# A spectral and dense two-layer program on one core: the shared SBUF region moved by 32 bytes, two transposes and the W2 loads reordered

## The chip, the cores and the metric

The kernel runs on one core of a Trainium2 chip. The metric is the device time of one execution in microseconds (us). Times of single instructions come from one profiled execution.

## The reference

Input x has 2048 rows of 1024 bf16 numbers. The program applies a spectral layer A, a dense layer B, and both once more with the same weights; each adds its result to x:

```
x = x + A(layernorm(x));  x = x + B(layernorm(x))      # twice
A(x): irfft2(rfft2(x) * (w_r + 1j*w_i))                # 2048 x 513 complex weights
B(x): h = x @ w1 + b1                                  # 1024 x 3584
      (h * tanh(softplus(h))) @ w2                     # mish, then 3584 x 1024
```

## The kernel before, in words

x stays in SBUF as XS, 16 tiles of 128 rows. Everything else, in both layers, lives in one shared region, ARENA; `alloc` cuts buffers out of it by hand-written byte offsets, and a new buffer inherits the waits of what lay there. ARENA is the last tensor that `build` reserves, so its start follows from the sizes of the small tensors ahead of it, of which EPS (a constant for the square root and a scratch word) and PAD1 (not used) are the last two. `W1_OFF`, where the W1 ring and the filter ring lie, is counted back from the region's end.

Each engine has a program of its own in the order in which the Python code adds operations; the code works out which semaphores each must wait for. So the order of the text is the order on each engine and on each DMA queue. Most loads are issued by SyncE (SP).

Layer A is a Fourier transform made of matmuls. In the first application the normalised x is never written; x is loaded a second time in a transposed order (XR, 32 loads of 128 KB with rows of 256 bytes) and multiplied with tables scaled by each row's factor (MN, `scaled`). Stage by stage for 8 groups, s2, s3, i1 and i2 follow. The result of each group is written to DRAM (`u_scratch`) and read back transposed into UT, in rows of 256 bytes (`u_turn`, `u_back`). The last matmuls of layer A, `i4`, need all of UT; they belong to the dense layer's code and are mixed into it.

Layer B takes the 2048 rows as four chunks of 4 tiles, c = 0 to 3. For each tile a layernorm is made (statistics on VectorE or, with `stats_act` and `sums_to_mv`, on ScalarE; `scales` is a chain of small VectorE operations; `apply` writes the normalised tile xn). For chunks 0 and 1, `transposed` makes 8 TensorE transposes of a tile (L933) into one bank, and VectorE copies the bank to XT (L938). `mm1(c, fg)` is 2 x 8 matmuls (L963) with a W1 tile, into three banks in turn, each followed by ScalarE's Mish (L967); a third argument takes half of the chunk's columns. After an `mm1` of chunk 1 the next W1 tile is loaded over the one just read. `mm2(c, t, h)` sums 28 matmuls (L981) over all tiles of W2, and VectorE adds the bank to XS (L986).

Chunks 0 and 1 are worked on in rounds, fg = 5 to 16. Each round has an `mm1` of chunk 0 (to fg = 13), one of chunk 1 (three tiles behind), `rest(3)`, and up to three loads of W2 tiles. `rest(n)` does n of the 16 units of i4 that make XS tiles 8 to 15: unit nb is 8 small matmuls (L888) into bank 3 + nb % 3, emptied by VectorE (L902). W2 tiles 16 to 27 lie in space that is free; tiles 0 to 15 lie where UT is, so they are loaded only in rounds that come after the last unit:

```
            rest(3)
            for _ in range(3):
                if w2_order and (w2_order[0] >= 16 or self.nb == 16):
                    load_w2(w2_order.pop(0))
```

After the rounds the first `mm2` waits for all 28 tiles of W2. SyncE then also issues the transposes by DMA for chunks 2 and 3 (`turned`).

Of the kernel before, what the change touches and what calls it, by code (L numbers as in the profile page):

```python
# [9 lines left out]
F32 = dt.float32  # L10
# [164 lines left out]
def to_bf16_bits(a):  # L175
    u = np.ascontiguousarray(a, dtype=np.float32).view(np.uint32).astype(np.uint64)
    return np.ascontiguousarray((((u + 0x7FFF + ((u >> 16) & 1)) >> 16) & 0xFFFF).astype(np.uint16))


class KB:  # L180
# [122 lines left out]
    def build(self):  # L303
        nc = self.nc
        tabs = make_tables()
        con = {k: nc.inline_tensor(to_bf16_bits(v), name=f"c_{k.lower()}") for k, v in tabs.items()}
        self.con = {k: v.ap().bitcast(BF) for k, v in con.items()}
        self.con["IDF"] = nc.inline_tensor(np.eye(P, dtype=np.float32), name="c_idf").ap()
        self.u_d = nc.dram_tensor("u_scratch", (8, P, 16, P), BF, kind="Internal").ap()
        self.w_d = nc.dram_tensor("w_scratch", (8, P, 2, 2, 512), BF, kind="Internal").ap()  # L310
        self.xn_d = nc.dram_tensor("xn_scratch", (16, P, self.D), BF, kind="Internal").ap()
        from contextlib import ExitStack
        with ExitStack() as es:
            def sb(name, shape, dtype=BF):
                return es.enter_context(nc.sbuf_tensor(name, [P] + shape, dtype))

            sb("PAD0", [64])
            self.XS = sb("XS", [16, self.D])
            self.IDENT = sb("IDENT", [P])
            self.M = sb("M", [P])  # L320
            self.MT = sb("MT", [P])
            self.FD = sb("FD", [5 * 512])
            self.BD = sb("BD", [13 * P])
            self.B1 = sb("B1", [self.NF], F32)
            self.B1h = sb("B1h", [self.NF])
            self.BN = sb("BN", [16, 12], F32)
            self.MV = sb("MV", [16, 2], F32)
            self.RS = sb("RS", [4, 16], F32)
            self.EPS = sb("EPS", [2], F32)
            sb("PAD1", [92])  # L330
            self.PS = es.enter_context(nc.psum_tensor("PS", [P, 8, 512], F32))
            self.PSb = self.PS[:].bitcast(BF)
            self.arena_bytes = nc.sbuf_bytes_remaining // 64 * 64 - 64
            self.ARENA = es.enter_context(nc.sbuf_tensor("ARENA", [P, self.arena_bytes // 2], BF))
            self.r_bank = [Res(f"bank{i}") for i in range(8)]
            self.r_xs = [Res(f"XS{i}") for i in range(16)]
            self.r_mv = [Res(f"MV{i}") for i in range(16)]
            self.r_rs = [Res(f"RS{i}") for i in range(16)]
            self.r_ident, self.r_m, self.r_mt, self.r_fd, self.r_bd = (Res(n) for n in ("id", "m", "mt", "fd", "bd"))
            self.r_b1, self.r_eps, self.r_warm = Res("b1"), Res("eps"), Res("warm")  # L340
            self.r_ud = [Res(f"ud{i}") for i in range(8)]
            self.r_wd = [Res(f"wd{i}") for i in range(8)]
            self.r_xnd = [Res(f"xnd{i}") for i in range(16)]
            self.npair = 0
            self.W1_OFF = self.arena_bytes - 4 * 4096
            self.layout()
            self.prologue()
            self.layer_A(0)
            self.layer_B(0, last=False)
            self.layer_A(1)  # L350
            self.layer_B(1, last=True)
            self.dma_wait_all()
            for p in (self.pe, self.dve, self.act, self.sp, self.pool):
                p.sem = es.enter_context(nc.semaphore(name=f"sem_{p.name}"))
            for d_ in self.dsems.values():
                d_.sem = es.enter_context(nc.semaphore(name=d_.name))
            self.block = es.enter_context(nc.Block())
            self.flush()
# [557 lines left out]
    def layer_B(self, li, last):  # L916
# [6 lines left out]
        def transposed(c, t, xn, eng=None):  # L923
            bank = 6 + nt[0] % 2
            nt[0] += 1
            xn.unread = False
            if t == 0:
                if XT[c % 2] is None:
                    XT[c % 2] = self.alloc(f"XT{c % 2}", self.ob[f"XT{c % 2}"], [8, 512])
                XT[c % 2].res.begin()  # L930
            fns = []
            for db in range(8):
                fns.append(lambda e, db=db: e.transpose(PSb[:, bank, db * P:(db + 1) * P], xn.ap[:, db * P:(db + 1) * P],  # L933
                                                        self.IDENT[:]))
            self.group(fns, reads=[xn.res, self.r_ident], writes=[self.r_bank[bank]])
            dst = XT[c % 2].ap[:, :, t * P:(t + 1) * P]
            src = PSb[:, bank, :].rearrange("p (a b) -> p a b", b=P)
            fn = (lambda e: e.activation(dst, src, ACT.Copy)) if eng is act else (lambda e: e.tensor_copy(dst, src))  # L938
            self.op(eng or dve, fn, reads=[self.r_bank[bank]], parts=[XT[c % 2].res])
# [11 lines left out]
        def mm1(c, fg, half=None):  # L951
            n = base + 14 * (c // 2) + fg
            wb = self.w1_buf[n % 6]
            x = XT[c % 2]
            tok = slice(0, 512) if half is None else slice(256 * half, 256 * half + 256)
            w = tok.stop - tok.start
            for fl in range(2):
                ft = 2 * fg + fl
                bank = nh[0] % 3
                nh[0] += 1  # L960
                fns = []
                for db in range(8):
                    fns.append(lambda e, db=db, bank=bank, fl=fl: e.matmul(  # L963
                        PS[:, bank, 0:w], wb.ap[:, db, fl * P:(fl + 1) * P], x.ap[:, db, tok], start=(db == 0), stop=(db == 7)))
                self.group(fns, reads=[wb.res, x.res], writes=[self.r_bank[bank]])
                at, ra = AT[c % 2], r_at[c % 2][ft]
                self.op(act, lambda e, bank=bank, ft=ft: e.activation(at.ap[:, ft, tok], PS[:, bank, 0:w], ACT.Mish,  # L967
                                                                      bias=self.B1[:, ft:ft + 1]),
                        reads=[self.r_bank[bank], self.r_b1], writes=[ra])
            if c % 2 and half != 0 and self.w1_next == n + 6 and n + 6 < base + 28:  # L970
                self.load_w1()
# [36 lines left out]
        def load_w2(ft):  # L1008
            W2[ft] = self.alloc(f"W2_{ft}", self.ob["W2"] + ft * 2048, [self.D])
            self.dma(sp, W2[ft].ap, w2v[:, ft, :], f"w2_{ft % 4}", writes=[W2[ft].res])  # L1010
# [5 lines left out]
        xn = {}  # L1016
# [3 lines left out]
        def at_tiles(c):  # L1020
            off = self.ob[f"AT{c}"]
            AT[c] = self.alloc(f"AT{c}", off, [NF, 512])
            r_at[c] = [Res(f"AT{c}_{ft}") for ft in range(NF)]
            for ft, r in enumerate(r_at[c]):
                r.inherit(AT[c].res)
                self.live.append((off + ft * 1024, off + ft * 1024 + 1024, r))

        def rest(n):

            for _ in range(n):  # L1030
                if self.nb == 0:
                    for j in range(8, 16):
                        self.r_xs[j].begin()
                if self.nb < 16:
                    self.i4(8, 8, 8 * self.nb, 8, 3 + self.nb % 3)
                    self.nb += 1
# [37 lines left out]
        for fg in range(4):  # L1074
            mm1(0, fg, 1)
            if fg in (1, 3):
                self.stats_act(6 + fg // 2)
        self.sums_to_mv(6, 2)
        self.scales(6, 2)
        for j in (6, 7):  # L1080
            xn[j] = self.apply(j)
        mm1(0, 4)
        at_tiles(1)
        for j in (4, 5):
            transposed(1, j - 4, xn[j])
        for fg in range(2):
            mm1(1, fg, 0)
        for j in (6, 7):
# [5 lines left out]
        for fg in range(5, 14 + 3):  # L1094
            if fg < 14:
                mm1(0, fg)
            mm1(1, fg - 3)
            rest(3)
            for _ in range(3):
                if w2_order and (w2_order[0] >= 16 or self.nb == 16):  # L1100
                    load_w2(w2_order.pop(0))
# [68 lines left out]
```

## Time and profile before

| what | us |
|---|---|
| three runs: median (lowest, highest) | 1082.23 (1076.47, 1083.42) |
| the profiled execution | 1081.24 |
| its span, from the first to the last instruction | 1079.4 |
| TensorE busy in it (PE) | 959.7 |
| VectorE busy (DVE) | 350.9 |
| ScalarE busy (ACT) | 339.5 |

The span is cut into instructions by engine; us in all rows count from the span's start. Idle time of TensorE is what an edit can give back; idle time of the others costs nothing by itself. The mean granted clock of TensorE was 0.96 of full speed.

### The profile page before, as it was taken

Reading aid. Unit: us, or ns where it says so; the run is one execution under the profiler, and the core shown is the slowest. Engines: PE = TensorE matmul, PEld = TensorE weight load, DVE = VectorE, ACT = ScalarE, POOL = GpSimd, SP = SyncE. Lnnn points to the kernel's source line nnn. Section 1 sums busy time; section 2 is a strip of 40 time slices with the busy share of each in tenths; the row PEclk is TensorE's granted clock in tenths of the full one; section 3 lists DMA queues with packets and bytes.
Section 4 is the critical chain, followed back from the end, with each engine's and each line's share of the span. In section 5 each row is a group of like instructions: output and inputs, shape, how many; then the busy total and the mean of one; then the engine's idle time right before and its main releaser. Section 6 shows DMA issues by size and latency. Waiting matters only on the chain. (4 is left out here: it accounts for less than half of the span.)

```text
span 1079.4 us, 14332 instructions
## 1 busy us (share of the span) xinstructions
PE 959.7 (89%) x6063; PEld 521.2 (48%) x6153; DVE 350.9 (33%) x775; ACT 339.5 (31%) x504; POOL 64.1 (6%) x102
## 2 busy tenths in 40 slices
PE   0699478998999999999967984899989999999998
PEld 0588375543444444444425754654434444444443
DVE  7877463250343200023325775413401110000111
ACT  6798344332000233400006863533300013441000
POOL 2042000000000000000520200000000000000000
PEclk9899779998999999999988995999999999999999
DMA  9969941446111122000951798044621112200000
GB/s 280 153 221 277 176 119 40 155 157 203 44 46 40 40 78 59 1 10 20 197 96 21 199 206 185 1 138 154 220 59 36 53 46 78 79 1 10 20 20 30
DMA packets 158480, 107.04 MB, mean 99 GB/s; under 512 B 80432, under 2 KB 138032, under 8 KB 158416
## 3 DMA queue, kind: packets, MB, share of 16 engines
q1 hardware_dynamic: 146272, 77.57, 28.2%
q0 software_dynamic: 9056, 26.87, 9.6%
q10 hardware_dynamic: 3088, 1.67, 0.9%
q8 instruction: 49, 0.80, 0.3%
q14 instruction: 15, 0.12, 0.0%
HBM read 80.85 MB, written 20.71 MB: 94 GB/s over the span
## 5 line engine op out<-in xcount | busy, mean ns | idle before, releaser
L963 PE MATMUL PS<-ARENA 128*128 128x512 bf16 (+1 forms) x1946 | 392.4, 361 | 14.2 <-DVE ARENA L938 11.0
L981 PE MATMUL PS<-ARENA 128*128 128x512 bf16 x1756 | 388.4, 381 | 8.5 <-DMA ARENA<-in_B_w_dram 6.6
L967 ACT ACTIVATE ARENA<-PS,B 128x512 bf16<-128x512 f32 (+1 forms) x248 | 159.6, 645 | 449.8 <-PE PS L963 449.8
L963 PEld LDWEIGHTS PS<-ARENA 128*128 128x128 bf16 x1984 | 194.3, 99 | 205.4 <-DVE ARENA L938 12.6
L981 PEld LDWEIGHTS PS<-ARENA 128*128 128x128 bf16 x1792 | 175.9, 98 | 220.8 <-issue 11.5
L986 DVE TENSOR_TENSOR XS<-PS,XS 128x512 bf16<-128x512 f32 x64 | 44.3, 692 | 517.0 <-PE PS L981 517.0
L453 DVE BATCH_NORM_STATS2 BN<-XS 128x6 f32<-128x512 bf16 x104 | 67.2, 675 | 7.5 <-DMA XS<-in_A_x_dram 6.3
L902 DVE TENSOR_TENSOR XS<-PS,XS 128x512 bf16<-128x512 f32 (+1 forms) x40 | 29.5, 791 | 110.8 <-PE PS L888 110.8
L888 PE MATMUL PS<-MT,ARENA 128*128 128x32 bf16 (+1 forms) x768 | 23.9, 187 | 32.7 <-DMA ARENA<-u_scratch 30.5
L888 PEld LDWEIGHTS PS<-MT,ARENA 128*128 128x128 bf16 x768 | 23.3, 101 | 36.2 <-issue 33.2
L434 ACT ACTIVATE ARENA<-XS 128x1024 bf16<-128x1024 bf16 x24 | 25.3, 1055 | 43.2 <-DVE XS L902 38.2
L708 ACT ACTIVATE ARENA<-PS 128x1024 bf16<-128x1024 f32 x32 | 33.0, 1032 | 9.1 <-PE PS L704 9.1
L663 PE MATMUL PS<-FD,ARENA 128*128 128x256 bf16 (+1 forms) x312 | 32.5, 252 | 2.4 <-DVE ARENA L590 2.4
L737 ACT ACTIVATE ARENA<-PS 128x1024 bf16<-128x1024 f32 x32 | 33.0, 1031 | 3.7 <-PE PS L730 3.7
L730 PE MATMUL PS<-ARENA 128*128 128x256 bf16 x256 | 33.2, 273 | 0.1
L425 ACT ACTIVATE RS<-MV,EPS 128x1 f32<-128x1 f32 (+1 forms) x7 | 2.0, 292 | 98.5 <-DVE MV L456 96.2
L249 POOL DMA_DIRECT2D xn_scratch<-ARENA x15 | 8.3, 554 | 401.5 <-DVE ARENA L492 401.5
L712 DVE TENSOR_TENSOR ARENA<-ARENA 128x1024 bf16<-128x1024 bf16 x32 | 22.1, 690 | 27.7 <-ACT ARENA L708 22.4
L730 PEld LDWEIGHTS PS<-ARENA 128*128 128x128 bf16 x256 | 24.6, 98 | 9.9 <-DVE ARENA L719 0.9
L663 PEld LDWEIGHTS PS<-FD,ARENA 128*128 128x128 bf16 x312 | 25.9, 98 | 6.8 <-DVE ARENA L590 2.8
L492 DVE TENSOR_SCALAR ARENA<-XS,MV,RS 128x1024 bf16<-128x1024 bf16 x48 | 25.0, 543 | 5.5 <-DMA xn_scratch<-ARENA 4.5
L751 PE MATMUL PS<-ARENA,BD 128*128 128x256 bf16 x192 | 25.9, 273 | 0.4 <-DVE ARENA L777 0.2
(69 smaller groups left out, 509.3 us busy)
## 6 DMA issues: line engine op xcount, KB each, us to landing
ARENA<-in_B_w_dram SPq DMA_DIRECT2D x56, 512.0 KB, 4.3
ARENA<-in_B_w_dram SPq DMA_DIRECT2D x56, 256.0 KB, 4.6
u_scratch<-ARENA SPq DMA_DIRECT2D x14, 512.0 KB, 3.9
ARENA<-u_scratch SPq DMA_DIRECT2D x14, 512.0 KB, 7.3
XS<-in_A_x_dram SPq DMA_DIRECT2D x4, 1024.0 KB, 8.7
ARENA<-in_A_x_dram SPq DMA_DIRECT2D x32, 128.0 KB, 5.2
w_scratch<-ARENA POOLq DMA_DIRECT2D x8, 512.0 KB, 5.4
ARENA<-w_scratch POOLq DMA_DIRECT2D x8, 512.0 KB, 5.5
```

Source lines behind the costliest of these rows:

```text
L453: self.op(self.dve, lambda e: e.bn_stats(self.BN[:, j, 6 * h:6 * h + 6], self.XS[:, j, 512 * h:512 * h + 512]), reads=[self.r_xs[j]], part ...
L663: fns.append(lambda e: e.matmul(dst, at(r), FD[:, t:t + dst.shape[-1] * 2], start=start, stop=stop))
L708: self.op(act, lambda e: e.activation(x.ap.rearrange("p a b -> p (a b)"), ps, ACT.Copy, scale=SIG), reads=banks, writes=[x.res])
L730: fns.append(lambda e, c=c, part=part: e.matmul(ps[:, c * 256:(c + 1) * 256], yk.ap[:, part, c * P:(c + 1) * P], t[:, (128, 0)[part]:(384, ...
L737: self.op(act, lambda e: e.activation(v.ap[:, :, i, :], src, ACT.Copy), reads=banks, parts=[v.res])
L751: fns.append(lambda e, dst=dst, part=part, c=c: e.matmul(dst, BD[:, c:c + P], mov(kd, part), start=(part == 0), stop=(part == 1)))
L888: fns.append(lambda e, l=l: e.matmul(ps[:, w * l:w * l + w], self.UT.ap[:, u0 + l, :], self.MT[:, 8 * lo:8 * lo + w], start=True, stop=True))
L902: self.op(self.dve, lambda e: e.tensor_tensor(xs, src, xs, ALU.add), reads=rb, parts=self.r_xs[lo:lo + nb])
L963: fns.append(lambda e, db=db, bank=bank, fl=fl: e.matmul(PS[:, bank, 0:w], wb.ap[:, db, fl * P:(fl + 1) * P], x.ap[:, db, tok], start=(db ...
L967: self.op(act, lambda e, bank=bank, ft=ft: e.activation(at.ap[:, ft, tok], PS[:, bank, 0:w], ACT.Mish, bias=self.B1[:, ft:ft + 1]), reads= ...
L981: fns.append(lambda e, i=i, ft=ft: e.matmul(PS[:, bank, :], at.ap[:, ft, t * P:(t + 1) * P], W2[ft].ap[:, h * 512:(h + 1) * 512], start=(i ...
L986: self.op(dve, lambda e: e.tensor_tensor(xs, PS[:, bank, :], xs, ALU.add), reads=[self.r_bank[bank]], writes=[self.r_xs[j]])
```

## The change

Three edits. EPS becomes 32 numbers long and PAD1 shorter, so that ARENA starts at another address. In layer B the two transposes of tiles 4 and 5 (the second chunk's first) and the `mm1` ahead of them move in front of the sums, scales and applies of tiles 6 and 7. And a round takes four units of i4.

```
-            self.EPS = sb("EPS", [2], F32)
-            sb("PAD1", [92])
+            self.EPS = sb("EPS", [32], F32)
+            sb("PAD1", [32])
...
+        mm1(0, 4)
+        at_tiles(1)
+        for j in (4, 5):
+            transposed(1, j - 4, xn[j])
         self.sums_to_mv(6, 2)
         self.scales(6, 2)
         for j in (6, 7):
             xn[j] = self.apply(j)
-        mm1(0, 4)
-        at_tiles(1)
-        for j in (4, 5):
-            transposed(1, j - 4, xn[j])
         for fg in range(2):
             mm1(1, fg, 0)
...
-            rest(3)
+            rest(4)
```

## Rows read from the trace of the kernel before

**Rows 1.** The page, part 1: busy us, share of the span, instructions.

```profile
PE 959.7 (89%) x6063; PEld 521.2 (48%) x6153; DVE 350.9 (33%) x775; ACT 339.5 (31%) x504; POOL 64.1 (6%) x102
```

**Rows 2.** Busy us by engine in windows; then granted clock, DMA share, GB/s.

```profile
core 0: us, PE busy (x) PEld busy (x) DVE busy (x) ACT busy (x) POOL busy (x), PEclk, DMA share, GB/s
...
23.20:51.30 28.10, 14.14 (x129) 12.97 (x129) 23.62 (x90) 21.94 (x56) 0.00 (x0) 0.82 1.25 188
...
120.20:135.50 15.30, 0.04 (x2) 0.07 (x3) 0.39 (x1) 1.02 (x1) 0.00 (x0) 0.57 1.14 195
...
556.30:572.60 16.30, 0.01 (x1) 0.04 (x2) 2.30 (x5) 0.29 (x1) 4.45 (x6) 0.59 0.45 80
...
643.50:657.90 14.40, 0.00 (x0) 0.01 (x1) 0.00 (x0) 1.02 (x1) 0.00 (x0) 0.65 1.15 197
```

**Rows 3.** Timeline of TensorE, second application, transposes: start, us, [idle before <-releaser].

```profile
693.10 1.06 PE L933 MATMUL PS<-IDENT,ARENA 128*128 128x128 bf16 x16
697.01 3.67 PE L963 MATMUL PS<-ARENA 128*128 128x256 bf16 x32 [2.85 <-DVE ARENA L938]
700.52 1.06 PE L933 MATMUL PS<-IDENT,ARENA 128*128 128x128 bf16 x16
702.51 3.67 PE L963 MATMUL PS<-ARENA 128*128 128x256 bf16 x32 [0.94 <-DVE ARENA L938]
```

**Rows 4.** The same timeline, first application, one row.

```profile
174.59 3.67 PE L963 MATMUL PS<-ARENA 128*128 128x256 bf16 x32 [2.86 <-DVE ARENA L938]
```

**Rows 5.** Timeline of VectorE, second application, around the same gap.

```profile
692.57 0.17 DVE L445 TENSOR_SCALAR MV<-BN 128x4 f32<-128x4 f32 x1 [2.89 <-ACT ARENA L434]
...
694.75 1.00 DVE L492 TENSOR_SCALAR ARENA<-XS,MV,RS 128x1024 bf16<-128x1024 bf16 x2
695.67 1.28 DVE L938 COPY ARENA<-PS 128x1024 bf16<-128x1024 bf16 x2
```

**Rows 6.** Timeline of TensorE, first application, end of the rounds.

```profile
228.76 31.24 PE L963 MATMUL PS<-ARENA 128*128 128x512 bf16 x141
263.06 37.17 PE L981 MATMUL PS<-ARENA 128*128 128x512 bf16 x155 [3.06 <-DMA ARENA<-in_B_w_dram]
```

**Rows 7.** The chain that ended last, second application; one TensorE row of the timeline.

```profile
775.15 3.85 PE PS L963 x17
...
779.43 6.43 DMA ARENA<-in_B_w_dram
...
785.99 3.61 PE PS L981 x16
...
785.99 20.23 PE L981 MATMUL PS<-ARENA 128*128 128x512 bf16 x91 [3.56 <-DMA ARENA<-in_B_w_dram]
```

**Rows 8.** SyncE's load in the fg = 14 round, both applications: issue, time to landing.

```profile
L249 SPq DMA_DIRECT2D ARENA<-in_B_w_dram x1: 581/581/581, 253.6 to 253.6; - x1
...
DMA to landing us min/median/max: 5.5/5.5/5.5
...
L249 SPq DMA_DIRECT2D ARENA<-in_B_w_dram x1: 582/582/582, 776.0 to 776.0; - x1
...
DMA to landing us min/median/max: 5.9/5.9/5.9
```

**Rows 9.** One round: chain (TensorE), timeline of VectorE, and L902's durations (ns).

```profile
713.09 0.71 PE PS L888 x24
...
713.84 6.85 PE PS L963 x31
...
713.36 1.89 DVE L902 TENSOR_TENSOR XS<-PS,XS 128x512 bf16<-128x512 f32 x3 [10.90 <-PE PS L888]
...
L902 DVE TENSOR_TENSOR XS<-PS,XS x16: 680/681/692, 190.9 to 229.0; 128x512 bf16<-128x512 f32 x16
```

**Rows 10.** DMA pace in 40 slices: one UT load (112.2 to 115.5), loads of x (30 to 42).

```profile
GB/s 28 137 251 286 285 298 298 276 295 292 285 273 174 177 171 158 168 152 155 158 149 146 168 149 158 152 149 158 155 143 155 146 115 248 28 19 0 0 0 0
...
GB/s 166 162 160 156 159 154 156 168 177 186 175 168 160 160 157 157 154 161 171 186 178 166 170 166 159 155 156 159 164 177 183 180 167 166 158 155 156 156 158 171
```

## The prediction

> **What bounds the kernel now.** I read the totals first: TensorE is busy for 959.7 of 1079.4 us [rows 1], so only what stands in the other 120 us, or what adds TensorE work, can move the time. The windows come next, because they say in which stretches TensorE stands still and what runs there: a start (23.2 to 51.3 us, TensorE busy 14.14 of 28.10), the tail of each spectral layer (120.2 to 135.5 and 643.5 to 657.9, TensorE busy 0.04 and 0.00, the DMA engines' share over 1), and the seam between the two halves (556.3 to 572.6, DMA share 0.45) [rows 2]. All the rest of the idle time is short gaps inside the dense layer, and two of the three edits aim at those: the timeline of TensorE shows a gap of 2.85 us ahead of the second chunk's first matmuls, and one of 3.06 and 3.56 us ahead of the first L981 [rows 3, 4, 6, 7]. Both occur once in each of the two applications of the layer.
>
> **The move of the two transposes.** In the second application TensorE starts the 16 transposes of tiles 4 and 5 at 693.10 and can go on with the second chunk only at 697.01, after VectorE's copies: 3.91 us [rows 3]. The reason stands in VectorE's own order: it waits for ScalarE's sums of tiles 6 and 7, and from 692.57 to 695.75 does eleven small operations (sums, scales) and two applies for tiles 6 and 7; the copies that TensorE waits for start at 695.67 and take 1.28 us [rows 5]. With the copies ahead, VectorE is idle when the transposes are ready. What start-to-resume then takes is seen on the next pair, where the copies had nothing ahead of them: 700.52 to 702.51, 1.99 us [rows 3]. So 3.91 - 1.99 = 1.92 us. The first application shows the same gap, 2.86 us [rows 4], so twice that: 3.8 us.
>
> What is late next? The small operations now run behind the copies. The copies end 0.06 us before TensorE resumes, at about 695.04; plus 3.18 us (695.75 - 692.57, [rows 5]) the applies of tiles 6 and 7 end at 698.2. TensorE has the first half of the second chunk to do meanwhile, 697.01 to 700.52, that is 3.51 us, so it asks for the next transposes at 695.10 + 3.51 = 698.6. That covers it by 0.4 us; if it didn't, the loss would be the same few tenths. mm1(0, 4) comes earlier in the text but TensorE's and ScalarE's orders don't change, since only VectorE has the moved scales; at_tiles issues nothing.
>
> **W2 loads released sooner.** The chain of the second application reads: L963 until 779.0, a W2 load issued by SyncE at 779.43, landing after 6.43 us, and the first L981 at 785.99 [rows 7]. mm2 waits for all 28 tiles of W2, and the last one leaves in the fg = 15 round. Tiles 0 to 15 may go once 16 units of i4 are done; at three units a round that is in the sixth round (fg = 10), at four in the fourth (fg = 8). Since twelve free tiles go in the first four rounds, tiles 0 to 15 now go in fg = 9 to 14 and not in 10 to 15: the last load leaves one round earlier. SyncE's queue is in order and each round begins with a W1 load that waits for mm1(1, fg - 3), so one round earlier is one mm1 earlier, 16 matmuls. The load in that place is there in the trace of before: in the first application it is issued at 253.6 and lands 5.5 us later, 259.1; in the second 776.0 + 5.9 = 781.9 [rows 8]. The last mm1 ends at 263.06 - 3.06 = 260.0 and 785.99 - 3.56 = 782.4 [rows 6, 7]. Both loads then land 0.9 and 0.5 us before they are wanted, and both gaps go: 3.06 + 3.56 = 6.6 us. The W1 loads that the W2 loads now precede on SyncE's queue are wanted three rounds later, over 10 us, and a load lands in 4 to 6 us; the transposes by DMA behind them still start after the last mm1.
>
> **Four units a round.** The units use three banks in turn, so the fourth unit of a round needs the bank of the first, which VectorE must have emptied. In the trace a round of three takes TensorE 0.71 us from 713.09; VectorE's first eviction begins at 713.36 and takes 0.68 us, to 714.04 [rows 9]. The fourth unit would go at 713.80 and now goes at about 714.08: 0.28 us of waiting, in four rounds, in two applications: 8 x 0.28 = 2.2 us lost. The units themselves are only moved. The bound below is 0 (nothing shows a fourth unit), the bound above is 0.5 us each, 4 us. VectorE is idle for 10.90 us before such a round [rows 9], so the eviction starts at once.
>
> **The region's place.** Tensors start at multiples of 32 bytes, so an EPS of 8 bytes takes 32 and the shared region starts at 60192, which is 235 x 256 + 32; with the edit it starts at 60160 = 235 x 256. Its end stays, so it is 64 bytes longer and the buffers counted from its end (four of the W1 ring, the filter ring) move from 160 to 192 past a multiple of 256. No engine row changes by this that I could price; DMA writes may. The loads at stake have rows of 256 bytes and stand in the idle stretches: the transposed x at the start (4.2 MB), and the last loads of UT in each tail. Bound below: 0, as no row shows such a load into a place at a multiple of 256. Bound above: one UT load, running alone, moves 285 GB/s for its first microsecond and then about 155; the loads of x hold about 160 throughout [rows 10]. If the better place let all of it go at 285, the start could gain no more than VectorE lets it, 28.10 - 23.62 = 4.5 us [rows 2]; and each tail, which has to bring in two UT loads of 0.52 MB, 1.04 MB / 155 = 6.7 us against 3.7, 3.0 us. Together 10.5 us. I take 4.0: the load keeps 285 for a while at the old place, so the place alone does not set the pace, which keeps me well under the upper bound; but the fall to 155 is of something behind the reading side, and a row of 256 bytes that starts 32 late covers two blocks of 256 where it need cover one. At the seam the DMA share is only 0.45 [rows 2], so pace isn't the limit, and I count 0.
>
> The Trainium skill, "DMA: Bandwidth & Descriptors", section "How a descriptor splits into AXI transactions", says that a transfer is cut into transactions at multiples of 256 bytes and that one starting off such a multiple needs one more, and more beats. By it a row of 256 bytes at 32 past a multiple costs nine beats and not eight; as an estimate, a ninth off the slow loads would be some 5 us and the sum about 1068. No view of before can confirm it: there is no load of this kind at a multiple of 256.
>
> **Sum.** 3.8 + 6.6 - 2.2 + 4.0 = 12.2 us. The profiled execution took 1081.24 us for a span of 1079.4, and 1.8 us lie around it; 1081.24 - 12.2 = 1069.0 us. That execution is 1.0 us under the median of the three runs, 1082.23, which themselves spread over 7 us. One per cent, about what a measurement of this kernel can tell from no change, is 10.8 us, so 1071.4: the forecast lies just across it.
>
> **Rivals.** First, the place buys nothing: the 155 GB/s are a matter of rows of 256 bytes, wherever they start. For it: the pace of 285 at the old place. Then 8.2 us remain, 1073.0. Second, the place buys all that the bound allows: 8.2 + 10.5 = 18.7, 1062.5; against it, the tails are also waits of one transfer on another, which no pace removes. Third, a wait takes the place of one removed: the last W2 load still lands after the last mm1 because the loads crowd in the shared queue. The room is 0.5 us in the second application; if half of the 6.6 us stay, the time is 1072 with the gain of place and 1076 without. Fourth, slower: the fourth unit waits not for the first eviction but for the round's whole set, which a late VectorE could bring about. Three evictions take 1.89 us from 713.36 [rows 9], so the wait would be 1.45 us, eight times 11.6; against 3.8 + 6.6, and with no gain from the place, that ends at +1.2 us, 1082.4. It decides from 10.4 / 8 = 1.3 us a round, and an idle VectorE speaks against it.
>
> **How the numbers follow.** Forecast 0.43, no gain from the place 0.33, all of it 0.13, a new W2 wait 0.08, slower rounds 0.03. Range: from 1062 (the second rival) to 1076 (the third at its worst, and the first with 4 us lost in the rounds is 1075). Faster by over 1%, under 1071.4: nearly all of the forecast's share, the second rival and a little of the third, 0.54. Slower by over 1% needs 11 us that no row shows, 0.03; within 1% 0.43.
>
> **What will show it.** Transposes: the gap ahead of the second chunk's first matmuls falls from 2.85 to about 0.95 us, and the next one stays at 0.94. W2: no gap ahead of the first L981. Rounds: runs of 32 L888 with a wait of 0.3 us for L902 in them. Place: the loads of x run at over 170 GB/s, and the tails last under 14 us. The prediction is wrong if the tails and the start don't shorten at all (then 1073), or if a gap ahead of L981 stays.

## The result, and the profile after

The changed kernel takes 1054.63 us (median of four runs, 1053.58 to 1056.39); the kernel before, run beside it, 1082.57 us. The ratio is 0.9755, with a 95% interval of 0.9717 to 0.9794. The forecast was 1069.0 us in a range of 1062 to 1076, so the gain is 28 us where 12.2 were forecast, and the time lies under the range. The profiled execution took 1053.58 us for a span of 1051.8.

The page, part 1, of the kernel after answers to [rows 1]: TensorE's work is nearly the same, so almost all that went is idle time.

```profile
PE 957.5 (91%) x6063; PEld 520.6 (49%) x6153; DVE 350.4 (33%) x775; ACT 339.0 (32%) x504; POOL 64.0 (6%) x102
```

The windows of the kernel after, in the four stretches of [rows 2] and with their columns: start, first tail, seam, second tail.

```profile
23.20:46.30 23.10, 13.61 (x129) 11.73 (x129) 22.47 (x90) 21.49 (x56) 0.00 (x0) 1.00 0.94 210
115.20:127.10 11.90, 0.00 (x0) 0.02 (x1) 0.39 (x1) 1.02 (x1) 0.00 (x0) 0.66 1.05 250
541.20:550.70 9.50, 0.00 (x0) 0.01 (x1) 2.30 (x5) 0.29 (x1) 2.76 (x4) 0.73 0.42 78
621.80:633.70 11.90, 0.03 (x2) 0.06 (x2) 0.38 (x1) 1.02 (x1) 0.00 (x0) 0.60 1.05 251
```

The first row has the same 129 matmuls as before in 23.10 us, where 28.10 were needed; VectorE is now busy for 22.47 of them, and its timeline has no gap from 23.80 us on, so it sets the end. The tails are 3.3 us shorter each at 250 GB/s for 195. The seam is 9.50 us long where it was 16.30, and its DMA share is as low as before, 0.42 for 0.45.

The timeline of TensorE after, for [rows 3, 4, 6, 7 and 9]:

```profile
163.71 3.67 PE L963 MATMUL PS<-ARENA 128*128 128x256 bf16 x32 [0.94 <-DVE ARENA L938]
...
179.61 0.86 PE L888 MATMUL PS<-MT,ARENA 128*128 128x64 bf16 x24
180.80 0.41 PE L888 MATMUL PS<-MT,ARENA 128*128 128x64 bf16 x8 [0.32 <-DVE XS L902]
...
206.26 44.84 PE L963 MATMUL PS<-ARENA 128*128 128x512 bf16 x203
250.93 19.37 PE L981 MATMUL PS<-ARENA 128*128 128x512 bf16 x88
...
669.11 1.06 PE L933 MATMUL PS<-IDENT,ARENA 128*128 128x128 bf16 x16
671.10 3.67 PE L963 MATMUL PS<-ARENA 128*128 128x256 bf16 x32 [0.94 <-DVE ARENA L938]
674.60 1.06 PE L933 MATMUL PS<-IDENT,ARENA 128*128 128x128 bf16 x16
676.60 3.67 PE L963 MATMUL PS<-ARENA 128*128 128x256 bf16 x32 [0.94 <-DVE ARENA L938]
...
758.33 17.00 PE L981 MATMUL PS<-ARENA 128*128 128x512 bf16 x77
```

A gap stands in brackets behind its row; a row without brackets has none. Ahead of the second chunk's first matmuls 0.94 us are left in both applications, and nothing ahead of the first L981. Each round of four now has one wait of 0.32 us for L902.

The DMA pace of the kernel after, for [rows 10]: first the x loads (28 to 40 us, GB/s in 40 slices and packets), then one UT load (107.3 to 109.5 us).

```profile
GB/s 251 132 154 244 147 185 167 202 192 154 213 194 243 191 242 202 236 142 125 224 174 245 178 244 153 254 165 207 202 153 237 142 216 169 205 206 207 163 207 233
DMA packets 9419, 2.34 MB, mean 195 GB/s; under 512 B 9419, under 2 KB 9419, under 8 KB 9419
...
GB/s 224 261 279 289 298 298 284 289 293 293 275 298 289 289 298 293 289 289 289 289 284 298 279 298 298 284 237 214 214 209 191 223 186 158 452 61 42 28 14 0
```

The UT load holds about 290 GB/s for 1.4 us, over two thirds of its length, where it had fallen to 155 after a third. The x loads run at 195 GB/s with dips between the loads. TensorE still waits for some of them (up to 2.22 us), but VectorE no longer waits for TensorE, so their pace no longer sets the length of the start.

From the two traces, the places where the 27.6 us of the span went:

| where | forecast | measured |
|---|---|---|
| start (L663 begins at 51.34, then 46.33) | in the 4.0 | 5.0 |
| two tails (idle 15.3 and 15.2, then 11.95 and 11.92) | in the 4.0 | 6.6 |
| seam (idle 16.38, then 9.54) | 0 | 6.8 |
| transposes (idle 2.86 and 2.85, then 0.94 twice) | 3.8 | 3.8 |
| gaps ahead of L981 (3.06 and 3.56, then none) | 6.6 | 6.6 |
| rounds of four | -2.2 | -3.6 |
| L981 at half clock, first application | not counted | 2.9 |
| small differences elsewhere | 0 | -0.5 |

The region's place gave 18.5 us (the first three rows), where 4.0 were forecast and 10.5 held for the most.

### The profile page after: what moved, and what is told of

It reads as the page before. It is cut to its first block, busy times and chain, and to the rows that moved or that the text cites. A ratio compares the mean times of both kernels' runs of the same rounds, so it can differ in the third digit from the quotient of the medians.

```text
span 1051.8 us, 14327 instructions
## 1 busy us (share of the span) xinstructions
PE 957.5 (91%) x6063; PEld 520.6 (49%) x6153; DVE 350.4 (33%) x775; ACT 339.0 (32%) x504; POOL 64.0 (6%) x102
## 5 line engine op out<-in xcount | busy, mean ns | idle before, releaser
L981 PE MATMUL PS<-ARENA 128*128 128x512 bf16 x1756 | 385.5, 379 | 1.9
L981 PEld LDWEIGHTS PS<-ARENA 128*128 128x128 bf16 x1792 | 175.3, 98 | 211.4
L902 DVE TENSOR_TENSOR XS<-PS,XS 128x512 bf16<-128x512 f32 (+1 forms) x40 | 29.1, 790 | 82.0 <-PE PS L888 82.0
L663 PE MATMUL PS<-FD,ARENA 128*128 128x256 bf16 (+1 forms) x312 | 32.5, 252 | 2.8 <-DVE ARENA L590 2.8
L730 PEld LDWEIGHTS PS<-ARENA 128*128 128x128 bf16 x256 | 24.6, 98 | 10.5 <-PE PS L704 1.0
L663 PEld LDWEIGHTS PS<-FD,ARENA 128*128 128x128 bf16 x312 | 25.9, 98 | 7.2 <-DVE ARENA L590 3.2
```

The source lines that it names most:

```text
L663: fns.append(lambda e: e.matmul(dst, at(r), FD[:, t:t + dst.shape[-1] * 2], start=start, stop=stop))
L730: fns.append(lambda e, c=c, part=part: e.matmul(ps[:, c * 256:(c + 1) * 256], yk.ap[:, part, c * P:(c + 1) * P], t[:, (128, 0)[part]:(384, ...
L902: self.op(self.dve, lambda e: e.tensor_tensor(xs, src, xs, ALU.add), reads=rb, parts=self.r_xs[lo:lo + nb])
L981: fns.append(lambda e, i=i, ft=ft: e.matmul(PS[:, bank, :], at.ap[:, ft, t * P:(t + 1) * P], W2[ft].ap[:, h * 512:(h + 1) * 512], start=(i ...
```

## The experiments

The theory after the result: the place is worth some 18 us and the other two edits some 9; what counts is that the rows of 256 bytes that the loads of x and UT write start at a multiple of 256. Rivals: the gain comes from the other edits; 32 is a special offset, or a multiple of 128 is enough; one of the two loads carries it all.

**The parts by themselves.** One kernel has only the new place, one everything but it, one only the moved transposes, one only the rounds of four.

```
place_only, against before:        place_undone, against after:
-  self.EPS = sb("EPS", [2], F32)  -  self.EPS = sb("EPS", [32], F32)
-  sb("PAD1", [92])                -  sb("PAD1", [32])
+  self.EPS = sb("EPS", [32], F32) +  self.EPS = sb("EPS", [2], F32)
+  sb("PAD1", [32])                +  sb("PAD1", [92])

transposes_only, against before: mm1(0, 4), at_tiles(1) and the two transposes
ahead of sums_to_mv(6, 2), as in the change
four_units_only, against before:
-            rest(3)
+            rest(4)
```

> Only the region's place is changed. If the place alone shortens the start (51.3 to 46.3 us), the two tails (15.3 and 15.2 to 11.9) and the seam (16.4 to 9.5), these are 5.0 + 3.4 + 3.3 + 6.8 = 18.5 us, and the time is about 1064. If the seam's gain came instead from the other edits (work that arrives in another order there), the seam stays at 16.4 and the time is about 1071.

Measured: 1065.08 us, ratio 0.983 (0.9784 to 0.9875), 19 us under the kernel before in the same comparison. L663 begins at 46.39, the tails are 12.0 us each and the seam 10.19; the other gaps stay (2.85 us twice, 2.85 and 2.44 ahead of L981).

> The changed kernel with the region back at its old place: the two moved transposes and the rounds of four are left. If the place is worth 18.5 us, 1054.6 + 18.5 gives 1073. If the parts depend on each other, the time differs from that by over 3 us.

Measured: 1073.39 us, ratio 0.9894 (0.9846 to 0.9941). The tails are 15.3 and 15.2 us again, the seam 15.47, and L663 begins at 50.70. By the same three rows the place is worth 17.7 us from the kernel before to place_only and 17.0 from place_undone to the kernel after. The 18.5 of the table are thus good to about one us: in the four kernels at the old place the seam lasts 15.1 to 16.4 us.

> Only the two transposes are moved. The gap ahead of the second chunk's first matmuls falls from 2.85 to 0.94 us in both applications and nothing else changes: 1.9 us twice, 1079. If a later wait takes the place, the next gap (0.94) grows by as much and the time stays at 1082.6.

Measured: 1078.7 us, ratio 0.9954 (0.993 to 0.9977): both gaps are 0.94 us; those ahead of L981 stay, at 3.52 and 3.51 us (before 3.06 and 3.56).

> Only the rounds of four. Theory: the gaps of 3.06 and 3.56 us ahead of the first L981 go, eight waits of 0.32 us and some 0.14 us of restart each come in (3.7 us), and the 2.9 us of matmuls at half clock behind the first gap go too: 5.8 us, 1077. Rival: the half clock behind that gap is not the gap's doing, and stays: 2.9 us, 1080.

Measured: 1076.76 us, ratio 0.9947 (0.9916 to 0.9978): no gap ahead of L981, a granted clock of 1.00 in the 6 us behind it in both applications, and the eight waits of 0.32 us. So the half clock went with the gap. Taken alone, place, transposes and rounds give 19.0, 5.4 and 7.3 us (all against 1084.06), 31.6 in sum against 28 together; the single terms are known only to about 3 to 5 us, as the intervals say.

**Which offset.** The changed kernel with PAD1 longer by 32 or 64 numbers, so that ARENA starts 64 or 128 past a multiple of 256.

```
-            sb("PAD1", [32])
+            sb("PAD1", [64])      # place_64;  place_128: [96]
```

> The changed kernel with the region 64 bytes past a multiple of 256. Theory: a row of 256 bytes that crosses a multiple of 256 is what costs, so this is as slow as 32 past: tails of 15.3 us, seam about 15.5, 1073. Rival: a multiple of 64 is enough, and 32 was bad for being none: tails of 11.9, 1055.

Measured: one execution of 1068.49 us; tails 15.1 us, seam 14.86, L663 at 49.64.

> The changed kernel with the region 128 bytes past a multiple of 256. Theory of the crossing: as at 32 and 64, 1073, tails of 15.3. Rival, that the number of bytes past the multiple sets the price: clearly other tails than at 64. Rival, that a multiple of 128 is enough: 1055.

Measured: one execution of 1069.81 us; tails 17.3 and 14.7 us, seam 14.70, L663 at 49.47. So neither 64 nor 128 past is enough; the tails and the seam show it, since one execution each says little about the time. The pace of the x loads (30 to 42 us), first of place_64, then of place_128:

```profile
DMA packets 8688, 2.16 MB, mean 180 GB/s; under 512 B 8688, under 2 KB 8688, under 8 KB 8688
```

```profile
DMA packets 9329, 2.36 MB, mean 196 GB/s; under 512 B 9321, under 2 KB 9321, under 8 KB 9329
```

At 32 past it is about 165, so these loads get faster with the distance, and at 128 past the mean is as high as at the multiple. That mean flatters the place at 128, because at the multiple VectorE holds the stretch: the median landing of an x load is 5.2 us at 32 past, 5.0 at 64, 4.5 at 128 and 3.2 at the multiple, and at 128 the start is only 1.2 us shorter than in place_undone. The UT loads there are the slowest of all (median landing 7.9 us; 7.3 before, 5.5 after). One of them in place_128 (111 to 114 us, GB/s in 40 slices):

```profile
GB/s 109 55 328 328 109 61 55 181 242 297 287 280 300 290 283 294 290 287 297 181 143 137 113 130 126 109 133 130 123 116 126 123 116 123 123 130 119 126 116 130
```

It begins at about 290 and falls to about 124, where at 32 past it falls to 155. So the distance matters, and not only whether a row crosses a multiple: at 128 past the UT loads are slower than at 32 and the x loads faster. Why the two differ stays open.

**Which load.** Here the region stays at a multiple of 256, and one buffer in it starts 32 later (XR) or 32 earlier (UT, with the two buffers that share its edges).

```
xr_32:  -  self.o = dict(XR=0, ...          ut_32:  -  YS=56 * K, UT=64 * K, ... JUNK=54 * K)
        +  self.o = dict(XR=32, ...                 +  YS=56 * K - 32, UT=64 * K - 32, ... JUNK=54 * K - 32)
```

> The region stays at a multiple of 256, and XR alone, the transposed x, lies 32 bytes further. If the rows of 256 bytes that are written into XR make the start and the seam, both go back: the start to 51 us, the seam to 15.5 to 16.4, the tails stay at 11.9, 5.0 + 6.4 = 11.4 us, 1066. If the seam is bound by the reads of the stored xn tiles or by other buffers, it stays at 9.5 and the time is 1060.

> The region stays at a multiple of 256, and UT (with two work buffers of ScalarE and VectorE below it, which must make room) lies 32 bytes lower. If the rows of 256 bytes written into UT make the tails, both go back to 15.3 us, start and seam stay, 6.7 us, 1061.3. If the tails come from the writes to DRAM (read from another buffer), nothing moves, 1054.6.

Measured: xr_32 1065.61 us, ratio 0.9837 (0.9802 to 0.9873); ut_32 1063.49 us, ratio 0.9813 (0.9781 to 0.9846). Windows of xr_32, then of ut_32, each the start, first tail, seam and second tail in the order of time:

```profile
23.10:50.60 27.50, 14.05 (x129) 12.42 (x129) 23.51 (x90) 21.84 (x56) 0.00 (x0) 0.81 1.24 184
121.70:133.60 11.90, 0.03 (x2) 0.01 (x1) 0.46 (x1) 1.02 (x1) 0.00 (x0) 0.66 1.04 252
547.70:563.70 16.00, 0.01 (x1) 0.04 (x2) 2.30 (x5) 0.29 (x1) 4.42 (x6) 0.64 0.43 79
634.60:646.40 11.80, 0.00 (x0) 0.00 (x0) 0.34 (x1) 1.02 (x1) 0.00 (x0) 0.63 1.06 252
```

```profile
23.10:47.10 24.00, 14.02 (x129) 12.27 (x129) 23.21 (x90) 21.61 (x56) 0.00 (x0) 0.80 0.92 204
117.20:132.40 15.20, 0.00 (x0) 0.00 (x1) 0.41 (x1) 1.02 (x1) 0.00 (x0) 0.57 1.13 196
547.20:557.40 10.20, 0.00 (x0) 0.00 (x0) 2.74 (x5) 0.29 (x1) 2.76 (x4) 0.61 0.43 80
629.50:644.60 15.10, 0.00 (x0) 0.00 (x0) 0.40 (x1) 1.02 (x1) 0.00 (x0) 0.67 1.15 198
```

They part cleanly. XR 32 late brings back the long start and the long seam and leaves the tails; UT 32 early brings back the tails at 196 GB/s and leaves the rest. Against 1054.63 the two cost 11.0 and 8.9 us, together 19.8; place_undone costs 18.8. The interval of ut_32 overlaps the changed kernel's (0.9717 to 0.9794), so for it the tails decide. So it is the first byte of the written rows, and both loads carry it.

**The rounds and the gap ahead of L981.** Three more kernels start from the changed one.

```
five_banks:   -  self.i4(8, 8, 8 * self.nb, 8, 3 + self.nb % 3)
              +  self.i4(8, 8, 8 * self.nb, 8, 3 + self.nb % 5)
three_units:  -  rest(4)
              +  rest(3)
ring_at_256:  five_banks, and
              -  self.W1_OFF = self.arena_bytes - 4 * 4096
              +  self.W1_OFF = self.arena_bytes - 4 * 4096 - 128
```

> The changed kernel with the units of i4 in five banks in turn and not three, so that a fourth unit finds an empty bank. If the waits of 0.32 us for VectorE inside the rounds are what the fourth unit costs, all eight go, and the rounds get 8 x 0.46 = 3.7 us shorter: about 1051 us. Rival: banks 6 and 7 are still held by something else at that point, or the restart behind the wait is not the wait's: then 1054 to 1055.

Measured: 1051.1 us (six runs), ratio 0.9734 (0.9704 to 0.9763); the interval overlaps the changed kernel's, so the step is read from the trace. TensorE's timeline of five_banks, two rounds and the first L981:

```profile
190.10 1.10 PE L888 MATMUL PS<-MT,ARENA 128*128 128x64 bf16 x32
191.03 7.07 PE L963 MATMUL PS<-ARENA 128*128 128x512 bf16 x32
197.94 1.10 PE L888 MATMUL PS<-MT,ARENA 128*128 128x64 bf16 x32
...
251.60 10.74 PE L981 MATMUL PS<-ARENA 128*128 128x512 bf16 x49
```

The four units run through, and a round takes 197.94 - 190.10 = 7.84 us. In the changed kernel it takes 189.13 - 180.80 = 8.33, so the fourth unit's wait cost 0.49 us: the 0.32 of idle time and 0.17 of starting again. Eight times that is 3.9 us.

> The changed kernel with three units a round again. If four units a round are what takes the gaps ahead of the first L981 away, both return at 2.5 to 3.6 us, the eight waits of 0.32 us go, and L981 runs its first 6 us at a granted clock under 1.00 in at least one application: net 2 to 6 us more, 1057 to 1061. Rival: the region's place already made the W2 loads early enough, no gap, and the eight waits are gone: 1051.

Measured: 1059.06 us, ratio 0.9805 (0.9762 to 0.9848); this interval too overlaps the changed kernel's. In the trace the gaps are back, and the clock behind them is down. TensorE's timeline of three_units, and the windows of 6 us behind each gap:

```profile
252.51 3.71 PE L981 MATMUL PS<-ARENA 128*128 128x512 bf16 x10 [2.90 <-DMA ARENA<-in_B_w_dram]
...
762.38 12.80 PE L981 MATMUL PS<-ARENA 128*128 128x512 bf16 x52 [2.77 <-DMA ARENA<-in_B_w_dram]
...
252.51:258.51 6.00, 6.00 (x20) 2.38 (x21) 0.00 (x0) 0.00 (x0) 0.00 (x0) 0.72 0.24 57
762.38:768.38 6.00, 6.00 (x22) 2.44 (x23) 0.00 (x0) 0.00 (x0) 0.00 (x0) 0.76 0.24 60
```

From the first L981 to the end of the last it takes 291.93 and 291.65 us, against 290.24 in both applications of the changed kernel: 1.7 and 1.4 us more. So even with the region in place, the W2 loads need the fourth unit.

> The kernel with five banks, and the W1 ring and the filter ring moved by 128 bytes to a multiple of 256 as well. If the place of a load counts only where TensorE waits for that load, nothing moves: within 0.3% of the kernel with five banks, about 1051. Rival: these loads take up DMA time that the others lack, and a better place for them gives another 2 to 4 us: 1047 to 1049.

Measured: 1051.18 us (six runs), ratio 0.9728 (0.9698 to 0.9757), no different from five_banks. The loads of W1 and of the filter aren't waited for, or their rows of 512 bytes don't gain; the run doesn't tell these apart, but nothing is to be had there.

## Why the prediction was wrong: the place of the region

**The transposes** were right in size and mechanism: 3.8 us forecast, 3.8 measured. VectorE's timeline after, second application, with the copies ahead of the sums and scales:

```profile
669.75 1.29 DVE L938 COPY ARENA<-PS 128x1024 bf16<-128x1024 bf16 x2 [4.07 <-PE PS L933]
670.96 0.16 DVE L445 TENSOR_SCALAR MV<-BN 128x4 f32<-128x4 f32 x1
...
673.13 1.00 DVE L492 TENSOR_SCALAR ARENA<-XS,MV,RS 128x1024 bf16<-128x1024 bf16 x2
675.25 1.29 DVE L938 COPY ARENA<-PS 128x1024 bf16<-128x1024 bf16 x2 [1.12 <-PE PS L933]
```

VectorE now waits 4.07 us for TensorE where TensorE waited for it. The applies of tiles 6 and 7 end at 674.13, and TensorE asks for them at 674.60: a cover of 0.47 us, forecast 0.4.

**The W2 loads** were right: both gaps went, and the last load is issued at 244.6 and lands after 5.0 us, 1.3 us ahead of the first L981 (1.5 in the second application), where 0.9 and 0.5 were forecast. Not foreseen was what the gap drew after it. The 6 us behind it, first of the kernel before, then of the one after:

```profile
263.06:269.06 6.00, 6.00 (x15) 2.09 (x16) 0.00 (x0) 0.00 (x0) 0.00 (x0) 0.51 0.22 49
```

```profile
250.93:256.93 6.00, 6.00 (x29) 2.74 (x28) 0.00 (x0) 0.69 (x1) 0.00 (x0) 1.00 0.39 109
```

With a granted clock of 0.51, nearly the lower level of 1.2 GHz throughout, TensorE did 15 matmuls where it later did 29. From the first L981 to the last the phase took 293.15 us before and takes 290.24 now: 2.9 us. In the second application of the kernel before, a longer gap (3.56 us) cost nothing of the kind: the clock in the 6 us behind it was 1.00. The six gaps of 2.4 to 3.5 us in place_only, transposes_only and three_units were followed by 0.72 to 0.76. What decides among these stays open. So a gap of some 3 us there costs 0 to 2.9 us more than itself.

**The rounds of four** had the right mechanism and too small a size: 0.28 us was forecast for each, 0.49 measured (five_banks); the wait itself is 0.32, and the other 0.17, which I left out, goes with it when the wait goes. Over the two applications that is 1.4 to 1.7 us.

**The region's place** is the step that failed, the term "I take 4.0" with its bound of 10.5, and the 0 at the seam; together they measured 18.5. Three steps of the reasoning went wrong: the choice between the ends, the bounds, and the seam.

The choice between the ends. I argued that the place alone doesn't set the pace because one load keeps 285 GB/s for a while at the old place. In ut_32 a UT load that is off the multiple, and alone on the DMA engines, does the same (109.2 to 112.5 us, GB/s in 40 slices):

```profile
GB/s 41 162 248 282 292 285 292 292 295 292 285 261 199 164 177 149 161 152 152 152 152 155 161 155 149 155 158 146 152 155 152 134 96 53 34 16 199 0 0 0
```

It runs at about 290 GB/s for 0.8 us and then at 134 to 177, about 155. So a fast beginning says nothing about the place; the sustained part does, and it was about 155 where it is now about 290. The other half of my argument held and should have weighed more: ut_32 reads the same bytes from DRAM and, of the loads, moves only where these bytes are written, and the fall is back.

The bounds. The start gave 5.0 us for at most 4.5, because I subtracted too much. The window of 28.10 us holds 0.79 us of VectorE's next copies, which TensorE doesn't wait for:

```profile
50.51 2.66 DVE L868 COPY ARENA<-ARENA 128x1024 bf16<-128x1024 bf16 x4
```

Without them the bound is 28.10 - 22.83 = 5.3 us. TensorE's clock, 0.82 before and 1.00 after, isn't the reason: in place_only it was 0.80, and L663 began at 46.39 as well. The tails gave 3.3 us each for 3.0; where the 0.3 come from wasn't followed up. The signs that I had named (x loads over 170 GB/s, tails under 14 us) came, and with all of the bound the second rival still stood at 1062.5.

The seam. I counted 0, because the DMA share is only 0.45 there. That was the wrong place to look: the seam's length was decided before it began. What TensorE waits for at its end are copies of the last tile within SBUF (`xr_direct`), here before, then after:

```profile
572.59 7.61 PE L582 MATMUL PS<-M,ARENA 128*128 128x128 bf16 x96 [16.38 <-DMA ARENA<-ARENA]
```

```profile
550.72 9.24 PE L582 MATMUL PS<-M,ARENA 128*128 128x128 bf16 x112 [9.54 <-DMA ARENA<-ARENA]
```

Two of them are issued by GpSimd, behind its 15 loads of xn into XR. GpSimd's queue ahead of the second application, first of the kernel before (the last L981 ends at 556.2), then of the one after (541.2):

```profile
516.54 7.69 POOL L249 DMA_DIRECT2D ARENA<-xn_scratch  x7
...
543.90 0.60 POOL L249 DMA_DIRECT2D xn_scratch<-ARENA  x1
551.10 1.08 POOL L249 DMA_DIRECT2D ARENA<-xn_scratch  x1 [6.60 <-DMA xn_scratch<-ARENA]
...
557.51 1.08 POOL L249 DMA_DIRECT2D ARENA<-xn_scratch  x1 [4.74 <-DMA xn_scratch<-ARENA]
...
565.52 1.08 POOL L249 DMA_DIRECT2D ARENA<-xn_scratch  x1 [6.31 <-DMA xn_scratch<-ARENA]
566.59 1.14 POOL L249 DMA_DIRECT2D ARENA<-ARENA  x2
```

```profile
501.52 7.67 POOL L249 DMA_DIRECT2D ARENA<-xn_scratch  x7
...
524.41 0.61 POOL L249 DMA_DIRECT2D xn_scratch<-ARENA  x1
530.19 1.08 POOL L249 DMA_DIRECT2D ARENA<-xn_scratch  x1 [5.17 <-DMA xn_scratch<-ARENA]
...
535.95 1.08 POOL L249 DMA_DIRECT2D ARENA<-xn_scratch  x1 [3.86 <-DMA xn_scratch<-ARENA]
...
541.74 1.08 POOL L249 DMA_DIRECT2D ARENA<-xn_scratch  x1 [4.13 <-DMA xn_scratch<-ARENA]
544.36 1.15 POOL L249 DMA_DIRECT2D ARENA<-ARENA  x2 [1.53 <-DVE ARENA L492]
```

The queue is in order. First come the loads of tiles 0 to 11, begun 39.7 us ahead of the end of the last L981 in both kernels. Then, for each of tiles 12 to 14, xn is stored to DRAM, the load of it transposed into XR waits for that store to land, and the next store stands behind that load. Before, the twelve loads took the queue 27.4 us (516.54 to 543.90), and the three turns behind them 21.6 us; now it is 22.9 and 17.3. So the last load went out 9.3 us after the end of the last L981 and now goes out 0.6 us after it, and the copies behind it now wait for VectorE and no longer for the queue. While the twelve loads ran, the DMA engines' share was 1.03 before and 0.95 after: their pace did count, only ahead of the gap. The 15 loads into XR landed after 10.8 us in the median before and 8.1 after, after 10.0 in xr_32 and 8.1 in ut_32, and xr_32 has the same stall again (turns up to 8.3 us, seam 16.0). That the place of XR sets the seam is shown by xr_32 and ut_32; that it does so by way of this queue is read from the traces.

**The page's rule.** The Trainium skill, "DMA: Bandwidth & Descriptors", section "How a descriptor splits into AXI transactions", had the direction right. Its figure, given for bytes that are fetched, is too small here, where only the place of writing moved: as an estimate, nine beats for eight would raise the UT load's 155 GB/s to 174, and it ran at about 290. By the same rule a row 128 past a multiple costs more beats than one 32 past; the x loads show the opposite (196 and 165 GB/s), the UT loads agree (7.9 and 7.3 us to landing, 124 and 155 GB/s). The measurements decide.

One sentence of mine on the change was wrong without effect: the region's length stays the same, and the buffers counted from its end move from 160 to 128 past a multiple of 256, not to 192.

## What to carry to other kernels

Where a DMA writes rows of 256 bytes into SBUF, look at the address of the first byte, the tensor's start plus the offset in it: small tensors declared ahead of it can shift all rows, and 32 bytes were worth 1.7% here (place_only, 1.2 to 2.2%), at no cost. To size such an edit, take the sustained pace of a load and not its first microsecond, and follow each in-order queue back past the stretch where the engine stands still: a low DMA share in a gap doesn't say that DMA pace has no part in it. A wait inside a run of matmuls costs more than the idle time shown, here 0.49 us for a gap of 0.32, and up to 2.9 us of half clock behind one of 3.

## What the runs showed of the hardware

The same load (UT, rows of 256 bytes) runs at about 155 GB/s when its rows start 32 past a multiple of 256 in SBUF, at about 124 when they start 128 past, and at about 290 for most of its length when they start at one; 64 past is no remedy either (median landing 6.9 us, where it is 7.3 at 32 and 5.5 at the multiple). It runs at about 290 for its first 0.8 us at the worse places too. The granted clock in the 6 us behind a gap of about 3 us ahead of L981 differed between applications of one kernel, 0.51 behind 3.06 us and 1.00 behind 3.56, and was 0.72 to 0.76 behind six such gaps of three other kernels.
